# A written-out order of some 5,400 operations is replaced by another, and the last tile leaves in one transfer

## The chip, the core and the metric

One NeuronCore of a Trainium2 chip runs the whole program. It has five engines with a queue of instructions each: TensorE (PE, matrix products), VectorE (DVE), ScalarE (ACT), GpSimd (POOL) and SyncE (SP, which here only issues transfers). The metric is the device time of one execution in microseconds, the median of several runs.

## The reference: banded and pooled attention, then a maxout layer

Attention runs over 8 batches, 8 heads, 576 positions of 64 numbers. The local part lets each position see only its neighbours at a distance under 4. The pooled part averages q, k and v over groups of 4 positions, runs full attention on the 144 averages, and repeats each result 4 times. Their sum, 4608 tokens of 512 numbers, goes through three products, their elementwise maximum, and an output product.

```python
q_d = q.reshape(B, H, Sd, factor, D).mean(axis=3)      # factor 4, Sd 144
out_d = sm_attn(q_d, k_d, v_d)
out_up = np.repeat(out_d, factor, axis=2)
mask = np.abs(pos[:, None] - pos[None, :]) < factor
scores = np.where(mask, scale * np.matmul(q, k.transpose(0, 1, 3, 2)), -1e9)
out_local = np.matmul(softmax(scores), v)
x = (out_up + out_local).transpose(0, 2, 1, 3).reshape(B * S, H * D)
h = np.maximum(np.maximum(x @ w1, x @ w2), x @ w3)     # 512 -> 768
return h @ w_out                                       # 768 -> 512
```

## The kernel before

**The work.** The tokens are cut into nine blocks of 512: the first 512 positions of each of the eight batches (blocks 0 to 7), and block 8, the last 64 positions of all eight. A block's attention is done in two groups of four heads, n = 2j and 2j+1. In blocks 0 and 1 the local attention runs on PE, in windows, with two head pairs a group; from block 2 on DVE, POOL and ACT do it by products, sums over seven offsets and multiplications. Two chains of the first part matter here. In `wide_scores` (L1264) PE opens two score banks with the mask (operations 24 and 25, 44 and 45, 84 and 85), adds the scores (26, 46, 86), DVE takes maxima, ACT exponentials, DVE sums and reciprocals (37 to 39), and one last multiplication in two halves (60 and 61 for the second pair of group 0, 124 and 125 for the first pair of group 1). In `wide_values` (L1308) PE transposes the result (64 to 67 and 69 for that pair, 174 to 179 for the other), a copy brings it to SBUF, and PE multiplies by v (71). `band_load` (L1133) brings the operands of a later group into tiles that are free by then: by the list `HOMES` (L64) both pairs of group 3 use the tile wlo4, so the loads 366 and 367 wait for the last readers of what lay there (the value products 383), the scores 389 read them, and the loads 369 and 370 of the next pair wait for 389 before the scores 390 can start. Pooled attention has its scores 132 to 139 and others, its pd transposes (489 waits for ptail, written by 483) and its products (454).

The maxout layer works with numbers split into a high and a low part; a product is three matmuls of 128x128 by 128x512 (`layer_one`, L1355). `mlp_column` (L1374) makes one of six columns of a block's hidden layer, `mlp_out` (L1400) its four output tiles y of 128 tokens: eighteen matmuls into one PSUM bank, a copy, a transfer to DRAM. Blocks 7 and 8 go through the maxout products together. There are four banks of tag pm, three of pa and one of pq.

**The order.** The kernel first records its operations as numbers, in the order in which the Python code names them, with what each needs (class Recorder); then `emit` (L723) issues them. Which engine does an operation and in what order stands in `TABLE` (L79), a list of words: a number or a range and a letter for the engine (P for PE, D for DVE, A for ACT, G for POOL, S for SP). `340D` is operation 340 on DVE, `24-25P` are 24 and 25 on PE. A word with F asks for so many filler matmuls: `20F` are 20 bf16 matmuls of the mask tile into a free bank, whose result nobody reads (`warm`, L705). `follow` (L617) goes through the list word by word and gives each new tile a place in SBUF or PSUM, the one that came free first by its own reckoning of times (`take`, `opens`, `ready`). So the list sets the order of each of the five queues and, through the places, who waits for whom.

```python
        for o, e in turn:
            if o is None:
                self.free[e], self.last_kind = self.warm(self.free[e]), "B"
                continue
            t = max(self.free[e], self.ready(o, e))
            for tag, infos in self.opens(o).items():
                places = sorted(self.freed[tag])[: len(infos)]
                assert len(places) == len(infos), (o.key, tag)
```

All instructions are issued by one line at the end of `emit`, L769, so the profile tells them apart by tile and shape only; which operation a row belongs to follows from its place in its engine's queue. Fillers show as rows whose only source is prod, 128x448 bf16. A load or store in the profile is a DMA named by its tile (v_1_0 and v_1_2 are loads of v for group 1, k_4_0 of k for group 4, traw_2_0 and rawin_1_1 of a tail and of a piece of w_in).

Of the kernel before, what the change touches and what calls it, by code (L numbers as in the profile page):

```python
# [79 lines left out]
11D 6S 8D 2D 4D 18D 3D 9S 5D 0D 7A 1D 10S 340D 884-885D 13-14S 126S 12S 129S 24-25P 167S 44P 21D 45P 169S 1F 26P 22D 19-20S 62D 42S 27D 46P 63D 28A  # L80
127G 16S 29-30A 17S 128G 34D 31A 47D 132P 43S 130G 32A 54D 33A 133P 197S 131G 48A 55D 134P 49A 168G 248S 50A 35D 135P 56A 140D 136-137P 170G 138-139P
51A 141D 52A 23S 142D 53A 171D 143A 36A 57D 238S 144A 58-59D 145A 60D 240S 61D 146A 6F 64-65P 37D 147A 66P 253S 73D 67P 69P 148A 258S 68A 74D 172G 70A
263S 149D 6F 71P 150D 155A 157D 278S 154D 173D 198G 152A 341S 151A 160P 199G 161P 72A 156D 162P 38D 158-159P 39D 163P 249D 165-166A 40D 200S 164A 41D
4F 75-76P 153D 1F 77P 15D 78P 250D 80P 84P 79A 85-86P 81A 342S 251A 82P 239D 87D 252D 268S 88A 105P 89A 106-107P 94D 241G 90A 346S 91A 83A 192P 95D
108D 242G 92A 115D 109A 203P 93A 288S 205P 116A 254D 193A 211D 194-195A 293D 196A 204P 110A 206P 111A 207-210P 112A 212D 296D 310S 113-114A 117A 213D
118A 214A 255D 315S 119A 259D 120-121A 260D 215A 96A 386S 122-123D 363D 216A 124G 97A 511S 217A 125D 20F 174P 414S 175P 98A 201D 176P 218A 177P 364D
202G 179P 449S 99A 219A 178D 100A 220D 180A 294A 221D 6F 181P 101-102D 451S 226D 228A 103G 225D 223A 227D 222D 104D 231P 297A 232P 229P 224D 295D 230P
# [1679 lines left out]
```

## Time and profile before

| what | us |
| --- | --- |
| median of 3 runs (690.0 to 691.69) | 690.52 |
| the profiled execution, its own time | 690.0 |
| its span in the trace | 688.2 |
| PE busy in the span | 675.5 (98%) |
| DVE busy | 627.1 (91%) |
| ACT busy | 400.9 (58%) |
| POOL busy | 361.9 (53%) |

The span is what the trace shows from the first to the last instruction; 1.8 us of the execution's time lie around it. A busy engine is not a useful one: the fillers count as busy. An engine's idle time matters only where it holds up the engine that the end hangs on.

### The profile page before, as it was taken

Reading aid. Unit: us, or ns where it says so; the run is one execution under the profiler, and the core shown is the slowest. Engines: PE = TensorE matmul, PEld = TensorE weight load, DVE = VectorE, ACT = ScalarE, POOL = GpSimd, SP = SyncE. Lnnn points to the kernel's source line nnn. Section 1 sums busy time; section 2 is a strip of 40 time slices with the busy share of each in tenths; the row PEclk is TensorE's granted clock in tenths of the full one; section 3 lists DMA queues with packets and bytes.
Section 4 is the critical chain, followed back from the end, with each engine's and each line's share of the span. In section 5 each row is a group of like instructions: output and inputs, shape, how many; then the busy total and the mean of one; then the engine's idle time right before and its main releaser. Section 6 shows DMA issues by size and latency. Waiting matters only on the chain.

```text
span 688.2 us, 12559 instructions
## 1 busy us (share of the span) xinstructions
PE 675.5 (98%) x4277; PEld 542.4 (79%) x4277; DVE 627.1 (91%) x855; ACT 400.9 (58%) x1352; POOL 361.9 (53%) x581
## 2 busy tenths in 40 slices
PE   6999999999999999999999999999999999999997
PEld 4678777878787788778877887788878888888885
DVE  7999999999999999999999999999998898999620
ACT  5875565658488547846684767556685654434121
POOL 2213137879599686839684968558356313332000
PEclk9999999999999999999999999999999999999999
DMA  9997455845355555445464635333430010000012
GB/s 307 402 314 234 130 166 183 241 129 191 114 159 170 176 173 165 140 145 171 155 172 133 188 121 158 85 112 108 146 98 19 1 61 1 1 0 1 1 61 61
DMA packets 50178, 92.79 MB, mean 135 GB/s; under 512 B 5540, under 2 KB 19426, under 8 KB 50114
## 3 DMA queue, kind: packets, MB, share of 16 engines
q1 hardware_dynamic: 49978, 91.86, 42.3%
q8 instruction: 33, 0.54, 0.3%
q14 instruction: 31, 0.25, 0.1%
q10 hardware_dynamic: 136, 0.13, 0.1%
HBM read 82.53 MB, written 9.44 MB: 134 GB/s over the span
## 4 chain that ended last, share of the span: by engine, by line
PE 89%; DVE 5%; ACT 2%; DMA 1%; issue 1%; SPq 0%; DVEq 0%
PE pm L769 75%; PE pa L769 13%; PE pq L769 2%; ACT prod L769 1%; DMA wlo<-in_kt_dense_dram 1%; ACT pa L769 1%; DMA whi<-in_qt_dense_dram 1%; DVE wlo_0r L769 1%; DVE t L769 0%; DVE hqk L769 0%; DVE sums L769 0%; DVE hh L769 0%; DVE xlo_0r L769 0%; DVE prod L769 0%; DVE qkT L769 0%
## 5 line engine op out<-in xcount | busy, mean ns | idle before, releaser
L769 PE MATMUL pm<-xlo_0r,whi_0r 128*128 128x512 f32 x540 | 211.8, 394 | 0.3 <-DVE xlo_0r L769 0.3
L769 PE MATMUL pm<-xhi_0r,wlo_0r 128*128 128x512 f32 x540 | 211.5, 392 | 0.0
L769 PE MATMUL pm<-xhi_0r,whi_0r 128*128 128x512 f32 x540 | 211.2, 392 | 0.0
L769 ACT ACTIVATE pv<-v,sums 128x64 f32<-128x64 f32 x532 | 140.2, 414 | 28.0 <-DVE x L769 11.0
L769 POOL TENSOR_TENSOR pv<-v,sums 128x256 f32<-128x256 f32 x245 | 145.5, 700 | 6.3 <-DMA v<-in_v_dram 2.9
L769 PE MATMUL pm<-wo_0r,hh_0r 128*128 128x512 f32 x576 | 137.8, 393 | 0.0
L769 PEld LDWEIGHTS pm<-wo_0r,hh_0r 128*128 128x128 f32 x576 | 106.7, 188 | 22.4 <-issue 0.6
L769 PEld LDWEIGHTS pm<-xlo_0r,whi_0r 128*128 128x128 f32 x540 | 101.3, 188 | 22.8 <-issue 2.0
L769 PEld LDWEIGHTS pm<-xhi_0r,wlo_0r 128*128 128x128 f32 x540 | 101.4, 188 | 21.0 <-issue 0.5
L769 PEld LDWEIGHTS pm<-xhi_0r,whi_0r 128*128 128x128 f32 x540 | 101.4, 188 | 20.9 <-issue 0.6
L769 DVE TENSOR_TENSOR prod<-k,pq 128x1792 f32<-128x1792 f32 x56 | 112.2, 2004 | 0.5
L769 DVE TENSOR_REDUCE sums<-prod 128x28 f32<-128x1792 f32 x56 | 112.0, 2001 | 0.3
L769 DVE TENSOR_REDUCE x<-pv 128x256 f32<-128x1792 f32 x43 | 85.9, 2008 | 1.3 <-POOL pv L769 1.2
L769 ACT COPY y<-pm 128x512 f32<-128x512 f32 (+1 forms) x48 | 27.9, 585 | 50.8 <-PE pm L769 38.5
L769 ACT CAST hh_0r<-pm 128x512 fp32r<-128x512 f32 x47 | 27.8, 591 | 40.3 <-DVE pm L769 40.3
L769 POOL TENSOR_TENSOR x<-whi_0r,wlo_0r 128x512 f32<-128x512 f32 x16 | 22.8, 1437 | 47.4 <-DVE x L769 32.4
L769 POOL TENSOR_TENSOR pv<-pv 128x768 f32<-128x768 f32 (+1 forms) x26 | 40.4, 1552 | 2.2 <-ACT pv L769 1.1
L769 ACT COPY pq<-q 128x256 f32<-128x256 f32 x56 | 22.1, 395 | 25.9 <-DVE prod L769 23.3
L769 DVE TENSOR_TENSOR hh_0r<-pm,hh_0r 128x512 fp32r<-128x512 f32 x47 | 32.0, 681 | 1.6 <-ACT hh_0r L769 1.4
L769 POOL TENSOR_TENSOR hv<-v 128x128 f32<-128x128 f32 (+1 forms) x53 | 26.7, 513 | 12.7 <-DMA v<-in_v_dram 12.5
L769 DVE TENSOR_TENSOR pm<-pm,t 128x512 f32<-128x512 f32 x44 | 30.4, 691 | 2.7 <-PE pm L769 2.4
L769 ACT COPY t<-pm 128x512 f32<-128x512 f32 x42 | 24.9, 592 | 13.6 <-PE pm L769 13.3
(377 smaller groups left out, 1035.1 us busy)
## 6 DMA issues: line engine op xcount, KB each, us to landing
k<-in_k_dram SPq DMA_DIRECT2D x55, 320.0 KB
v<-in_v_dram SPq DMA_DIRECT2D x54, 320.0 KB
out_dram<-y SPq DMA_DIRECT2D x35, 256.0 KB
q<-in_q_dram SPq DMA_DIRECT2D x56, 128.0 KB
hqk<-in_qt_pool_dram SPq DMA_DIRECT2D x24, 256.0 KB
hqk<-in_kt_pool_dram SPq DMA_DIRECT2D x24, 256.0 KB
wo<-in_w_in_dram SPq DMA_DIRECT2D x8, 511.8 KB
hh<-in_w_in_dram SPq DMA_DIRECT2D x6, 511.8 KB
```

Of the source, the lines that this page charges most:

```text
L769: getattr(self.engines[o.eng], method)(*map(real, args), **{k: real(x) for k, x in kw.items()})
```

## The change

Three things change. `TABLE` is another list. In `follow` a filler is issued only if a bank of pm or pa is free at that place of the list. And `mlp_out` no longer cuts the last tile, y_8_3, in two (before: ACT copies the left half and issues its transfer, DVE copies the right half and SP issues its transfer); ACT copies it whole and SP sends it, as all others. Two operations fall away with that, 5390 and 5391.

```diff
@@ -629,7 +612,8 @@
         assert len(asked) == known == len(set(asked)), "the table is of another program"
         for o, e in turn:
             if o is None:
-                self.free[e], self.last_kind = self.warm(self.free[e]), "B"
+                if self.freed["PSUM", "pm"] or self.freed["PSUM", "pa"]:
+                    self.free[e], self.last_kind = self.warm(self.free[e]), "B"
                 continue
             t = max(self.free[e], self.ready(o, e))
             for tag, infos in self.opens(o).items():
@@ -1407,16 +1391,12 @@
             for m, (a, b) in enumerate(ops):
                 pe.matmul(ps, a, b, start=m == 0, stop=m == len(ops) - 1)
             y = new([P, DM], tag="y", bufs=2, name=f"y_{j}_{f}")
-            pieces = 2 if (j, f) == (B, FAC - 1) else 1
-            w = DM // pieces
-            for x in range(0, DM, w):
-                last = x > 0
-                (dve.tensor_copy if last else act.copy)(y[:, x : x + w], ps[:, x : x + w])
-                if j < B:
-                    dst = dram(out, (j * S + f) * DM + x, [[FAC * DM, P], [1, w]])
-                else:
-                    dst = dram(out, (FAC * P + f) * DM + x, [[S * DM, B], [FAC * DM, TAIL], [1, w]])
-                (act if pieces > 1 and not last else sp).dma_start(dst, y[:, x : x + w])
+            act.copy(y, ps)
+            if j < B:
+                dst = dram(out, (j * S + f) * DM, [[FAC * DM, P], [1, DM]])
+            else:
+                dst = dram(out, (FAC * P + f) * DM, [[S * DM, B], [FAC * DM, TAIL], [1, DM]])
+            sp.dma_start(dst, y)
 
```

The two lists begin as follows (the old one with its first nine lines of 193, the new one with its first seven of 176):

```diff
-11D 6S 8D 2D 4D 18D 3D 9S 5D 0D 7A 1D 10S 340D 884-885D 13-14S 126S 12S 129S 24-25P 167S 44P 21D 45P 169S 1F 26P 22D 19-20S 62D 42S 27D 46P 63D 28A
-127G 16S 29-30A 17S 128G 34D 31A 47D 132P 43S 130G 32A 54D 33A 133P 197S 131G 48A 55D 134P 49A 168G 248S 50A 35D 135P 56A 140D 136-137P 170G 138-139P
-51A 141D 52A 23S 142D 53A 171D 143A 36A 57D 238S 144A 58-59D 145A 60D 240S 61D 146A 6F 64-65P 37D 147A 66P 253S 73D 67P 69P 148A 258S 68A 74D 172G 70A
-263S 149D 6F 71P 150D 155A 157D 278S 154D 173D 198G 152A 341S 151A 160P 199G 161P 72A 156D 162P 38D 158-159P 39D 163P 249D 165-166A 40D 200S 164A 41D
-4F 75-76P 153D 1F 77P 15D 78P 250D 80P 84P 79A 85-86P 81A 342S 251A 82P 239D 87D 252D 268S 88A 105P 89A 106-107P 94D 241G 90A 346S 91A 83A 192P 95D
-108D 242G 92A 115D 109A 203P 93A 288S 205P 116A 254D 193A 211D 194-195A 293D 196A 204P 110A 206P 111A 207-210P 112A 212D 296D 310S 113-114A 117A 213D
-118A 214A 255D 315S 119A 259D 120-121A 260D 215A 96A 386S 122-123D 363D 216A 124G 97A 511S 217A 125D 20F 174P 414S 175P 98A 201D 176P 218A 177P 364D
-202G 179P 449S 99A 219A 178D 100A 220D 180A 294A 221D 6F 181P 101-102D 451S 226D 228A 103G 225D 223A 227D 222D 104D 231P 297A 232P 229P 224D 295D 230P
-233P 182A 234P 183-185P 888S 186P 237A 298D 188P 236A 187A 189D 264D 896S 235A 256A 5F 190P 265D 261A 257D 269D 266A 243P 886S 191A 262D 347P 546P
...
+6S 11D 8D 2D 4D 18D 3D 9S 5D 0-1D 10S 340D 884-885D 7A 13-14S 126S 12S 129S 24-25P 167S 44P 21D 45P 169S 22D 1F 26P 19-20S 62D 42S 46P 27D 16S 127G
+63D 17S 128G 28-29A 43S 34D 130G 30A 132P 197S 47D 31A 131G 133P 32A 54D 168G 248S 134P 33A 135P 55D 48A 170G 49A 136P 35D 137P 23S 50A 138P 141D 140D
+56A 36A 139P 52A 51A 53A 85P 84P 86P 171G 142D 37D 57D 38D 58D 39D 59D 61D 60D 94D 15D 172D 143-146A 173D 40-41G 69P 6F 64-65P 70A 147-148A 95A
+149-150D 157D 87D 66-67P 4F 75-76P 1F 77-78P 73-74G 198-199G 68A 100A 6F 71P 152D 155D 151D 154D 156D 153D 72D 99A 96-97A 79A 98A 160P 158-159P
+161-163P 105P 80P 88-89A 165A 164A 92A 90-91A 93A 249D 166D 250D 81D 251A 207P 106-107P 208-210P 192P 213D 101D 108D 115D 109D 116D 253S 254D 102-103D
+82P 83D 194A 193A 195-196A 112A 118A 117A 119-120A 114A 110-111A 121A 113A 204P 203P 205-206P 258S 259D 211-212D 104G 414S 415D 252D 122D 416D 123D
+260D 124D 268S 200S 240S 238S 125D 214-219A 269A 255D 220D 293D 221D 20F 174P 183-185P 179P 175-177P 186P 180A 178A 222A 294A 256A 187A 261A 225D 296G
...
```

They end as follows; 5299 to 5307 are the last nine matmuls of the tile y_7_3, 5308 and 5309 its copy and transfer, 5374 to 5387 belong to y_8_3:

```diff
-5354-5367P 5370-5371P 5368A 5372-5373P 5369S 5374-5387P 5390D 5388-5389A 5391S
...
+5343-5345P 5372P 5355-5358P 5346-5347P 5348A 5349S 5359P 5373P 5360-5361P 5374P 5362P 5375P 5363-5367P 5368A 5369S 5376-5380P 5297-5298P 5381-5387P
+5388A 5389S 5299-5307P 5308A 5309S
```

PE's list has the same 2843 operations in both, and 49 fillers; 312 operations change the engine (94 go from POOL to ACT, 81 from ACT to POOL, 48 from DVE to POOL, 44 from ACT to DVE, 30 from POOL to DVE, 15 from DVE to ACT).

## Rows read from the trace of the kernel before

**Rows 1.** Busy time by stretch: bounds, length, busy us of each engine, clock, DMA share, GB/s

```profile
11.00:40.00 29.00, 27.96 (x437) 18.49 (x438) 26.76 (x71) 25.46 (x112) 7.66 (x13) 1.00 1.03 388
40.00:72.00 32.00, 30.25 (x511) 24.19 (x510) 30.60 (x59) 18.07 (x31) 7.61 (x9) 1.00 0.77 255
72.00:116.00 44.00, 43.65 (x400) 33.72 (x399) 43.11 (x71) 27.59 (x78) 15.87 (x22) 1.00 0.48 144
116.00:683.00 567.00, 566.98 (x2840) 461.80 (x2839) 519.31 (x635) 325.05 (x1112) 327.87 (x529) 1.00 0.37 113
```

**Rows 2.** Timeline of PE around 11 us: start us, us, engine, line, operation, out<-in, count

```profile
10.91 2.20 PE L769 MATMUL pm<-prod 128*128 128x448 bf16 x6
```

**Rows 3.** Timeline of PE, 25 to 33 us

```profile
25.13 3.96 PE L769 MATMUL pm<-prod 128*128 128x448 bf16 x20
29.46 0.96 PE L769 MATMUL pm<-ident,prod 128*128 128x128 f32 x5 [0.38 <-POOL prod L769]
```

**Rows 4.** Waits of PE over the whole span: us in total, times, longest

```profile
PE pa L769 <- DMA wlo<-in_kt_dense_dram: 1.5, 1, 1.5
PE pm L769 <- ACT pa L769: 0.6, 1, 0.6
PE pm L769 <- POOL prod L769: 0.4, 1, 0.4
PE pm L769 <- DVE xlo_0r L769: 0.3, 1, 0.3
PE pa L769 <- ACT dtail L769: 0.3, 1, 0.3
```

**Rows 5.** Timeline of DVE, 12 to 14 us

```profile
13.15 0.89 DVE L769 TENSOR_TENSOR prod<-prod,zb 128x256 f32<-128x256 f32 x2
```

**Rows 6.** Timeline of PE, 58 to 72 us

```profile
58.18 0.21 PE L769 MATMUL pq<-prod,wlo 32*64 32x18 f32 x2
...
63.56 0.89 PE L769 MATMUL pa<-wlo 64*26 64x32 f32 x80
...
64.72 0.40 PE L769 MATMUL pm<-xhi_0r,wlo_0r 128*128 128x512 f32 x1
...
68.59 0.39 PE L769 MATMUL pm<-xhi_0r,whi_0r 128*128 128x512 f32 x1
70.44 0.86 PE L769 MATMUL pa<-wlo 64*26 64x32 f32 x80 [1.46 <-DMA wlo<-in_kt_dense_dram]
```

**Rows 7.** The chain of waits, 55 to 72 us: start us, us, what

```profile
64.93 5.38 DMA wlo<-in_kt_dense_dram
```

**Rows 8.** Timeline of PE around 108 us

```profile
108.39 0.30 PE L769 MATMUL pa<-ident,pd 128*128 128x128 f32 x1 [0.29 <-ACT dtail L769]
```

**Rows 9.** Groups by line and form: busy us, mean ns, idle time before

```profile
L769 DVE TENSOR_REDUCE x<-pv 128x256 f32<-128x1792 f32 x43 | 85.9, 2008 | 1.3 <-POOL pv L769 1.2
...
L769 POOL TENSOR_TENSOR pv<-pv 128x768 f32<-128x768 f32 x13 | 24.0, 1850 | 1.2 <-ACT pv L769 1.1
...
L769 POOL TENSOR_TENSOR pv<-pv 128x512 f32<-128x512 f32 x13 | 16.3, 1254 | 1.0
```

**Rows 10.** Timeline of DVE, 678 to 689 us

```profile
683.53 0.42 DVE L769 COPY y<-pm 128x256 f32<-128x256 f32 x1 [24.25 <-PE pm L769]
```

**Rows 11.** DMA share, 684 to 688 us, 40 slices of 0.1 us, digits in tenths

```profile
DMA  0000000000004444445555455546510000000000
```

**Rows 12.** Timeline of ACT, 667 to 689 us

```profile
667.20 0.59 ACT L769 COPY y<-pm 128x512 f32<-128x512 f32 x1 [1.79 <-PE pm L769]
...
679.44 0.59 ACT L769 COPY y<-pm 128x512 f32<-128x512 f32 x1 [3.49 <-PE pm L769]
683.99 0.37 ACT L769 COPY y<-pm 128x256 f32<-128x256 f32 x1 [3.96 <-DVE y L769]
```

**Rows 13.** DMA share, 680 to 684 us, as before

```profile
DMA  0000000000001846292503822245553564321000
```

**Rows 14.** DMA share, 667 to 671 us, as before

```profile
DMA  0000000000000000399989940000000000000000
```

More of the change, by code (lines that the diff above doesn't have):

```diff
@@ new lines @@
+1489A 1260A 1235P 955-956P 959A 1236-1244P 1232D 989D 1205A 1044G 999G 1001P 1274-1275P 1289-1292P 1003-1005A 1002A 1093A 1483D 1206D 1245D 1246A
+1096A 1247D 1091A 1051P 1054D 1053D 1052D 1095A 1090A 1276P 1261-1268P 1302P 1293P 1269-1270P 1277-1278P 1271P 1279-1281P 1272P 1490-1491D 1273D
+1282-1285P 1286D 1092G 1102G 1055A 1497A 1056-1060A 1294-1295P 1303-1304P 1296-1300P 1305-1311P 1287A 1104A 1301A 1330-1331P 1315-1318P 1332P
+1061-1062D 1064A 1063A 1496S 1498D 1066D 1068D 1067D 1333P 1072P 1070-1071P 1334P 1633G 1103G 1615-1616G 1100G 1607G 1634G 1608G 1097G 1094G 1598S
@@ new lines @@
+1398-1400P 1375P 1357-1366P 1075P 1453-1454P 1514A 1329D 1515D 1455D 1516D 1603A 1078A 1077A 1456A 1401P 1367P 1376P 1368D 1517G 1564G 1377-1378P
+1411P 1120P 1379P 1412-1415P 1124A 1121A 1380P 1416-1417P 1381P 1610S 2076S 1122A 1369A 1457D 1604D 1370D 1605D 1382P 1465-1466P 1383P 1418P
+1384-1385P 1419P 1431P 1386-1388P 1552S 1557A 1123A 2058S 1609S 1617S 1611A 1554A 1389A 1567A 1467-1468P 1469D 1470A 1559A 1568A 2043G 1555G 1612D
+1458P 1402P 1432-1436P 1403P 1472-1474P 1459-1461P 1475P 1462D 1471D 1476D 1437P 1420P 1404-1408P 1421P 1563G 1553G 1560G 1566G 2059G 1558G 1556G
@@ new lines @@
+1637G 1565G 1561D 1569G 1571G 1618S 1390S 2050S 871S 1422-1425P 1582S 1572S 1409A 1463A 1477A 1478D 2188S 2046S 1410S 1464D 1613D 1426-1428P 1619A
+1429A 1438P 1711-1712P 1714P 1713P 1715-1716P 1720P 1717P 1583G 1721P 1737P 1439-1445P 1722P 1446-1448P 1738P 1524P 1585A 1587A 1575A 1589A 1576A
+1449A 1620D 1526-1527D 1525D 1621D 1574G 2077G 1590G 1578-1579G 2078G 2060G 1573G 1584G 2044G 1580G 1625D 2051G 1626D 1739-1748P 1726-1728P 1732P
+1718P 1752P 1719P 1753P 1733-1734P 1723-1725P 1577A 1588A 1581D 1586A 2052G 1627G 1528-1533A 1628A 1729-1731P 1754P 1735A 1591D 1450S 2037S 2039A
@@ new lines @@
+1693G 1696G 1708G 2214G 2224G 1710G 2191S 2648S 2184S 2632S 2142S 2183S 2649G 1699G 1656D 2057D 2064-2065D 2069D 1875P 1868-1869P 1876-1877P
+1889-1891P 2185A 1859D 2070D 1870P 2082P 1892P 1878-1884P 1893-1897P 1885P 1871P 2226G 2633G 2227G 2634G 2199S 2152S 2079S 2071G 2080-2081G 1886P
+1901-1904P 1898-1899P 2186-2187D 2196S 2192S 2086A 1872D 1887A 2072A 2193A 2085A 2073D 2194D 2640S 1873A 2074D 1874D 1900D 1916-1918P 1905-1911P
+2087-2089P 1919-1920P 1912P 1921-1924P 2084A 2201A 1913D 1925P 1929P 1926-1927P 2115D 2195D 2075G 2197G 2149A 1928A 1930-1933P 1942P 1957P 2117D
@@ new lines @@
+3461G 3462A 3825A 3319A 3316-3318P 3321A 3293A 3294D 3826-3827D 3477G 3475G 3197-3198P 3481P 3492P 3189P 3320A 3476A 3471A 3464A 3482P 3190P 3496P
+3199-3201P 3497P 3202-3208P 3408P 3483P 3176S 3832S 3953S 3831S 3156S 3480G 3472G 3463G 3473-3474G 3479G 3410A 3409A 3833A 3415D 3413D 3467A 3469G
+3414D 3416-3418A 3209-3214P 3912S 3922S 3961S 3954S 3992S 3851G 3215A 3419-3420A 3412A 3487-3489P 3493-3495P 3499-3501P 3505A 3411A 3834-3835D
+3191-3193P 3955A 3421A 3498P 3507-3508P 3194P 3195A 3509-3510P 3502P 3511-3513P 3503P 3522-3523P 3514-3515P 3524P 3516P 3525-3526P 3504P 3517P
```

330 lines of the change are left out of this document (147 added, 183 removed).

## Prediction, made before the changed kernel was run

> **What bounds the kernel now.** I first read the busy time of each engine in six stretches, four of which matter [rows 1]. From 116 to 683 us TensorE (PE) is busy 566.98 of 567.00 us: whatever the other engines do there is covered, and the end moves only by what PE does in the first 116 us, by a new PE wait later, and by what follows its last matmul. From 11 to 116 us the same column leaves 1.0, 1.8 and 0.4 us idle. Busy is not useful, though: of the 29 us from 11 to 40, PE spends some 10 on matmuls that fill waits (the table's F words, rows with prod as the only source): six in 2.20 us at 10.91 and twenty in 3.96 us at 25.13 are the two ends of it [rows 2, 3]. So what can be won is the waits, and fills only where the list has fewer of them.
>
> The second view is who made PE wait [rows 4]: 1.5 us for a load into wlo, 0.6 us for a softmax, 0.4 us for POOL's product, 0.3 us each for the operand xlo and for a softmax tail. Beside these 3.1 us the view has only the waits for the first loads, before 11 us.
>
> **The change, part by part.** I read both tables as five queues, one per engine, and added the durations of the trace along them. PE's list holds the same 2843 operations and 49 fills, so PE's work is the same; some 310 operations go to another engine.
>
> *0 to 11 us.* PE's first fourteen operations, SP's first eighteen and DVE's first twenty-two stand as they did: 0.
>
> *11 to 40 us.* (a) Operation 60, half of a softmax's last multiplication, now stands on DVE behind 37, 38, 39 and 61 (1.41 us together) and no longer behind 171 (0.41 us, to POOL). It ended within the pair of 13.15 to 14.04 us [rows 5]; it ends 1.0 us later, and the transposes 64 to 67 of PE with it. In their place PE is given 85, 84 and 86, the three score operations of the next head pair, which stood after both groups of this pair's transposes and need nothing new: the time is used, not lost. (b) The next gate is operation 124, then 125: the product before the second group of transposes, for which PE waits at 29.46 us [rows 3]. Up to 125 DVE is given 16 operations of 6.25 us (score maxima, pd, pt, xb copies from ACT) and loses 11 of 5.99 us (to POOL, or to later places): 0.26 us more. Product 124 itself goes from POOL to DVE, where the pair of [rows 5] took 0.89 us together. PE has 20 fills ahead of it in both lists, so it stands there again, 0.2 us later. (c) One fill of the 49 falls out: at the second 1F all four pm and all three pa banks are held in list order, and the new condition skips it; 0.19 us, but PE then waits for 124 anyhow: 0. (d) SP's loads change places from the nineteenth on, while the DMA engines are full, 1.03 of their time [rows 1]; what is brought forward (traw_2_0, rawin_1_1) pushes v_1_0 and v_1_2 back by two loads, and their reader on DVE has itself gone back 34 places: 0. Sum +0.2 us; at best the waits of 0.6 and 0.4 us and the xlo wait beside them go (-1.3), at worst the 1.0 us of (a) comes back whole (+1.2).
>
> *40 to 72 us.* The wait for wlo is a chain of its own: the value products 383 end at 58.39 us and free the tile, two loads follow, and PE's scores 389 start at 63.56; they free the tile again, the second pair of loads ends in one that goes out at 64.93 and takes 5.38 us, and scores 390 start at 70.44 [rows 6, 7]. What PE has in hand meanwhile counts. Before: 21 matmuls and two 0.14 us bank openings, then 19 matmuls. After: 19, then 22, and the openings stand elsewhere. From start to start these take 0.228 us (17 from 64.72 to 68.59) [rows 6]. So the cover is 9.4 us before (40 matmuls and the openings) and 9.3 after (41). The first chain lasts 5.1 us, up to 389, if it only just came in time, as I take it. It is then no longer covered (4.3 us of matmuls: a new wait of 0.8), and the second wait shrinks from 1.46 to about 0.9: +0.2 us. Bounds: the first loads land early, within the cover that is left, and the second wait goes too (-1.6); or the k_4_0 load that now stands ahead of the second pair in SP's list takes its bandwidth (+1.0).
>
> *72 to 116 us.* The transposes 489 wait 0.29 us at 108.39 us [rows 8]. Before them stand 4.3 us more of PE work in the new list, and 1.1 us less of DVE work up to their last reader 483: the wait goes. The matmul before could have been followed 0.45 us earlier; with 0.15 us of the same kind at the products 454: -0.6 us. Bounds 0 and -0.9.
>
> *116 to 683 us.* Twelve sums over seven offsets go from DVE's one reduction, 2.01 us, to POOL's three additions, of which the first two take 1.85 + 1.25 us, all three some 4; 94 and 81 multiplications trade between POOL and ACT [rows 9]. DVE is freed of some 24 us of 519 and POOL gets 48 more on 328 of 567 [rows 1]: neither is near the end. PE reads what these sums make 8 us later at the least, most of it 40 us. 0; at worst one such wait for a late sum each in two blocks, +1.5.
>
> *The end.* Now PE ends with the tile y_8_3, and that leaves in two halves: DVE's copy starts at 683.53 us, ACT's follows (it reads the same bank), and the two transfers' last packets start at 686.9 to 687.0 us [rows 10, 11]. After, the list ends otherwise: y_8_3 is done nine matmuls, 2.05 us, before the last one, and those nine finish y_7_3, whose copy by ACT and transfer by SP stand last. Both go in one piece. Their prices are there: y_8_2, of y_8_3's form, is copied in 0.59 us by 680.03 and has its last packets at 683.6 to 683.7, 3.65 us later; y_7_3 itself is copied by 667.79 and has its last at 669.3 to 669.4, 1.55 us later [rows 12 to 14]. So y_8_3 ends at 683.53 - 2.05 + 0.59 + 3.65 = 685.7, and y_7_3, were it alone, at 683.53 + 0.59 + 1.55 = 685.7 too. They meet: y_8's rows keep the DMA engines less than half busy as a mean, y_7's 0.9 of them for 0.8 us [rows 13, 14], which I read as eight of sixteen against all. What y_7_3 has for those eight stands behind y_8_3 and adds up to 0.8 us; I take 0.7: 686.4 instead of 687.0, -0.6 us. Bounds -1.3 (they pass without touching) and +0.1 (the meeting costs twice that). One piece as such is no gain: the halves needed 3.0 us from the start of the second copy, 683.99 [rows 12], the whole 3.65 from the end of its one. [...]
>
> **Sum** against the profiled execution's own 690.0 us (688.2 of span and 1.8 around it): +0.2 + 0.2 - 0.6 + 0 - 0.6 = -0.8, 689.2. The median of the runs, 690.52, lies 0.5 above that execution, so I put the measured time at 689.7 us.
>
> **Rivals.** *The clock comes late (slower).* Fills at 10.91 us take 0.37 us each and those at 25.13 us 0.20 [rows 2, 3]: the first run at half speed, the 1.2 GHz level, though the column prints 1.00 there. PE was busy without a break ahead of that rise. In the new list it has 85, 84 and 86 there, then stands still for over a microsecond until operation 61 is done, and the fills come only behind 69. If it is still at the low level then, the 16 fills between 69 and 71 cost 0.17 us more each, 2.7 us, and pass it on through the copies of 71's banks to DVE and so to 124: 689.7 + 2.7 = 692.4. It decides if the fills behind 69 take 0.37 us. For it: that idle time. Against it: 84 to 86 are work too. The Trainium skill, TensorE: Matmul & The Clock Gate, Part 1, says that the slow clock is the resting state and that sustained activity lifts it; the trace agrees. Chance 0.13.
>
> *The load chain and the softmax waits go (faster).* If the wlo loads land early the 1.6 us go instead of +0.2, and with the 1.3 us of the stretch before instead of +0.2: 689.7 - 3.3 = 686.4. For it: the same pair one block earlier found an emptier queue, and DMA share falls to 0.77 in that stretch [rows 1]. Against it: the cover in matmuls is the same. Chance 0.25.
>
> *A new wait inside the covered stretch (slower).* Long accumulations now interleave over all four pm banks: operation 812 opens an output tile some 19 us of PE work early, and near the end 5310 opens y_8_0 only some 0.3 us after DVE's 5229 frees its bank, by the same sums. At a place like that one operation in the way, of 0.59 us as ACT's copies [rows 12], holds PE by 0.3 us or more; I count seven with less than 0.3 us to spare in the new list, one in the old: with 0.35 us at each, 689.7 + 2.5 = 692.2. It decides if the whole operation is in the way at each. Against it: the list has that room, and DVE is free 48 us of 567. Chance 0.1.
>
> **How the numbers follow.** The forecast, no change that can be told, has 0.52; its own range is the sum of the bounds taken as independent, 687.2 to 691.9. A measurement of this kernel tells about 0.3% (2.1 us) from no change: 688.4 to 692.6. The forecast gives 0.09 to faster and 0.02 to slower; the second rival's 0.25 goes to faster; the first and the third, at the edge of that band, give 0.11 of their 0.23 to slower and the rest to the same. That makes 0.34, 0.53 and 0.13. The range reaches from the second rival to the first: 686.3 to 692.5.
>
> **What would show it.** Right: PE's idle time before 390's scores split into two waits near 63 and 70 us; no wait at the pd transposes near 108; PE unbroken from 116 us; the last packets 2.9 us behind the last matmul. Wrong: fills of 0.37 us behind 14 us; a PE wait after 116 us; both wlo waits gone; last packets later than 3.3 us behind the last matmul.

## The result and the profile after: 1.2% slower, where no change was forecast

The changed kernel took 699.1 us as a median of 4 runs (696.01 to 699.88); the kernel before, beside it, 690.26 (689.3 to 691.69). The ratio is 1.0118 [1.0083, 1.0153]. The forecast was 689.7 us, the range 686.3 to 692.5: the measured time lies outside of it, on the slow side. The profiled execution shown here took 699.88 us with a span of 698.1, against 690.0 and 688.2 before.

The busy time of each engine by stretch, for the changed kernel; the columns are those of [rows 1]:

```profile
11.00:40.00 29.00, 26.82 (x353) 18.02 (x353) 26.04 (x74) 22.33 (x101) 8.97 (x13) 0.94 0.72 256
40.00:72.00 32.00, 31.15 (x590) 24.61 (x588) 28.91 (x55) 16.16 (x29) 6.90 (x7) 1.00 0.86 290
72.00:116.00 44.00, 41.06 (x361) 31.58 (x362) 40.56 (x70) 23.19 (x68) 21.15 (x26) 1.00 0.55 179
116.00:692.50 576.50, 573.28 (x2876) 460.61 (x2875) 512.37 (x646) 334.20 (x1148) 377.93 (x558) 1.00 0.36 112
```

PE (second number) is idle 2.2 us from 11 to 40 (1.0 before), 0.9 from 40 to 72 (1.8 before), 2.9 from 72 to 116 (0.4 before) and 3.2 behind 116 us (0.02 before). The clock of the first row is 0.94, not 1.00. Who made PE wait, from the view of waits (us in total, times, longest):

```profile
PE pm L753 <- DVE t L753: 3.3, 2, 2.6
PE pm L753 <- DMA prod<-in_band_dram: 3.1, 1, 3.1
PE pm L753 <- ACT pa L753: 1.9, 1, 1.9
PE pm L753 <- issue: 1.4, 1, 1.4
...
PE pm L753 <- DVE hh_0r L753: 1.2, 1, 1.2
PE pa L753 <- DVE qkT L753: 0.5, 1, 0.5
```

Against [rows 4]: the load into wlo (1.5) and the wait of 489 are gone. The second line is the first load, before 11 us, which the old kernel has too. The softmax's (third line) has grown from 0.6 to 1.9, and five new ones of half a microsecond or more have come: two on DVE's t, one on its hh_0r, one put down to its qkT, and one for nothing that is seen.

**At 14 us.** PE's timeline, then those of DVE and POOL, of the changed kernel:

```profile
11.25 0.79 PE L753 MATMUL pm<-pv 64*58 64x64 f32 x36
13.93 0.30 PE L753 MATMUL pm<-ident,prod 128*128 128x128 f32 x1 [1.89 <-ACT pa L753]
14.07 1.78 PE L753 MATMUL pm<-prod 128*128 128x448 bf16 x6
15.64 1.06 PE L753 MATMUL pm<-ident,prod 128*128 128x128 f32 x4
16.50 1.70 PE L753 MATMUL pm<-prod 128*128 128x448 bf16 x4
```
```profile
12.83 1.97 DVE L753 TENSOR_TENSOR prod<-prod,zb 128x384 f32<-128x384 f32 x2
```
```profile
12.80 1.71 POOL L753 TENSOR_TENSOR prod<-prod,zb 128x256 f32<-128x256 f32 x2 [1.13 <-DVE zb L753]
```

The transposition 69 starts 1.89 us after the score operations are through. The view names ACT, but what 69 reads is the half that operation 61 writes, the first of DVE's pair at 12.83 us. That pair took 0.89 us in the old kernel [rows 5], where POOL ran nothing from 12.43 to 14.82 us (its next operation there is the first line below); here POOL does 40 and 41 in the same two microseconds, and the pair takes 1.97, of which 61 alone 1.00 instead of 0.55. The sixth experiment (e6, below) has the new order at this place, but 40 and 41 on DVE behind the pair; there POOL is idle beside it, and the pair takes 0.89 again (second line).

```profile
14.82 0.46 POOL L769 TENSOR_TENSOR th<-traw 128x128 f32<-128x128 f32 x1 [2.39 <-DMA traw<-in_qkt_tail_dram]
```
```profile
13.57 0.89 DVE L753 TENSOR_TENSOR prod<-prod,zb 128x384 f32<-128x384 f32 x2
```

Behind the standstill the clock falls (stretch by stretch, clock in the third column from the end):

```profile
14.00:16.00 2.00, 2.00 (x9) 1.19 (x10) 2.00 (x5) 1.14 (x6) 1.92 (x4) 0.69 1.04 412
16.00:18.00 2.00, 2.00 (x9) 1.13 (x8) 1.93 (x7) 1.26 (x6) 1.44 (x4) 0.50 1.00 400
18.00:20.00 2.00, 2.00 (x19) 1.25 (x19) 0.59 (x5) 1.77 (x10) 0.00 (x0) 0.96 0.98 324
```

From 14.7 us PE runs 3.4 us at 0.50, the lower level, and the four fills at 16.50 take 0.37 us each to the next start.

**From 62 to 96 us**, PE's timeline:

```profile
64.12 1.14 PE L753 MATMUL pa<-wlo 64*26 64x32 f32 x80 [0.50 <-DVE qkT L753]
...
70.42 0.87 PE L753 MATMUL pa<-wlo 64*26 64x32 f32 x80
...
72.40 0.50 PE L753 MATMUL pm<-xhi_0r,whi_0r 128*128 128x512 f32 x1 [0.68 <-DVE t L753]
...
79.93 2.06 PE L753 MATMUL pa<-y,whi 32*64 32x26 f32 x128
81.82 0.63 PE L753 MATMUL pa<-prod,whi 32*64 32x26 f32 x32
82.38 0.73 PE L753 MATMUL pm<-xhi_0r,wlo_0r 128*128 128x512 f32 x2
84.50 0.39 PE L753 MATMUL pm<-xlo_0r,whi_0r 128*128 128x512 f32 x1 [1.39 <-issue]
...
94.98 0.50 PE L753 MATMUL pm<-wo_0r,hh_0r 128*128 128x512 f32 x1 [1.16 <-DVE hh_0r L753]
```

At 64.12 the scores 389 wait, as forecast (put down to DVE's qkT here; 0.6 us and put down to the load into wlo in e5, a second run of the same kernel). At 70.42 the scores 390 no longer wait at all, where about 0.9 us was forecast. Not forecast: 669 at 72.40 and 812 at 94.98 open a PSUM bank that DVE has yet to give back, and at 84.50 operation 700 stands 1.4 us with nothing to wait for that the profile shows ("issue"), two matmuls behind a burst of 160 small ones (410 and 411). What DVE does ahead of 812's bank:

```profile
90.26 2.01 DVE L753 TENSOR_TENSOR prod<-k,pq 128x1792 f32<-128x1792 f32 x1
92.31 2.02 DVE L753 TENSOR_REDUCE sums<-prod 128x28 f32<-128x1792 f32 x1
94.24 0.68 DVE L753 TENSOR_TENSOR hh_0r<-pm,hh_0r 128x512 fp32r<-128x512 f32 x1
```

The last of these is 709, the reader of the bank; the list puts 890 and 891 before it, 4 us of work.

**At 400 us**, DVE, POOL and PE:

```profile
396.55 4.02 DVE L753 TENSOR_TENSOR sums<-sums,mask 128x48 f32<-128x48 f32 x1
400.49 0.15 DVE L753 TENSOR_SCALAR rd<-pa 128x5 f32<-128x5 f32 x1
400.56 0.67 DVE L753 TENSOR_TENSOR t<-pm,t 128x512 f32<-128x512 f32 x1
```
```profile
396.26 0.75 POOL L753 TENSOR_TENSOR kd<-hqk 128x256 f32<-128x256 f32 x1
...
399.77 0.73 POOL L753 TENSOR_TENSOR vd<-hv 128x256 f32<-128x256 f32 x1
```
```profile
401.29 0.50 PE L753 MATMUL pm<-xhi_0r,whi_0r 128*128 128x512 f32 x1 [2.61 <-DVE t L753]
```

An operation on 48 columns (3395) is on record with 4.02 us while POOL runs seven operations without a break, and DVE's next reader of a PSUM bank, 3080 at 400.56, comes too late for PE. It is a single event: of nine other traces with this stretch of the list, the same operation took 0.20 us in eight and 0.74 in one.

**The end**, ACT's last copy and the DMA share from 694 to 698 us, 40 slices of 0.1 us:

```profile
693.96 0.58 ACT L753 COPY y<-pm 128x512 f32<-128x512 f32 x1 [1.45 <-PE pm L753]
```
```profile
DMA  7382421822346478999895464532000000000000
```

The last packets start at 696.7 us, 2.8 to 2.9 behind the last matmul's end at 693.88, as forecast. The trace ends 4.23 us behind that end; before it was 4.77 (683.44 to 688.21). The last matmuls after, then before:

```profile
691.68 2.20 PE L753 MATMUL pm<-wo_0r,hh_0r 128*128 128x512 f32 x9
```
```profile
679.65 3.79 PE L769 MATMUL pm<-wo_0r,whi_0r 128*128 128x512 f32 x16
```

**Where the time went.** PE is on the path nearly everywhere, so I took, from one PE operation's start to the next one's, what went beyond the time that the same operation took in the old trace (0.229 us at most for a 128x512 matmul, 0.19 for a fill) and added it up by stretch. A wait counts where the operation before it starts, in the time of its own trace: 669's, at 71.2 us in after and 71.3 in e5, stands in the row 40 to 72. Column e5 is the changed kernel run once more, unaltered; the other columns are experiments of the next section.

| us of PE beyond the work | before | after | e5 | e9 | e10 | e11 | e13 | e15 | e3 | e12 |
| --- | --- | --- | --- | --- | --- | --- | --- | --- | --- | --- |
| 0 to 11 | 1.9 | 1.8 | 1.9 | 2.5 | 2.0 | 1.6 | 2.3 | 3.4 | 1.9 | 1.5 |
| 11 to 40 | 2.5 | 3.9 | 3.9 | 2.5 | 5.0 | 3.2 | 2.9 | 1.9 | 2.5 | 2.7 |
| 40 to 72 | 3.2 | 3.1 | 3.3 | 3.7 | 5.1 | 3.6 | 3.6 | 3.1 | 3.2 | 2.1 |
| 72 to 100 | 1.0 | 4.0 | 4.6 | 4.9 | 3.3 | 5.9 | 3.1 | 4.6 | 1.1 | 2.3 |
| 100 to 116 | 1.1 | 0.4 | 0.3 | 0.6 | 0.4 | 0.4 | 0.5 | 0.3 | 1.1 | 0.8 |
| behind 116 | 6.9 | 14.2 | 11.8 | 11.0 | 10.9 | 11.0 | 11.9 | 9.6 | 10.8 | 6.9 |
| sum | 16.6 | 27.4 | 25.8 | 25.3 | 26.8 | 25.7 | 24.3 | 22.9 | 20.5 | 16.4 |

The sums close: after, 27.4 - 16.6 and -0.5 at the end make 10.3, where the two profiled executions differ by 9.9; for e5 9.2 - 0.6 = 8.6 against 8.4. The event at 400 us makes 3.1 us of after's last row (3.65 us from 380 to 410 us, against 0.55 in e5).

### The profile page after: what moved, and what is told of

Same layout as the page of the kernel before. It is cut to its first block, busy times and chain, and to the rows that moved or that the text cites. A ratio compares the mean times of both kernels' runs of the same rounds, so it can differ in the third digit from the quotient of the medians.

```text
span 698.1 us, 12535 instructions
## 1 busy us (share of the span) xinstructions
PE 680.2 (97%) x4276; PEld 539.8 (77%) x4276; DVE 615.1 (88%) x865; ACT 401.2 (57%) x1363; POOL 418.1 (60%) x612
## 5 line engine op out<-in xcount | busy, mean ns | idle before, releaser
L753 PE MATMUL pm<-xhi_0r,whi_0r 128*128 128x512 f32 x540 | 204.3, 397 | 3.5 <-DVE t L753 3.3
L753 PE MATMUL pm<-xhi_0r,wlo_0r 128*128 128x512 f32 x540 | 205.8, 394 | 0.0
L753 PE MATMUL pm<-xlo_0r,whi_0r 128*128 128x512 f32 x540 | 202.0, 395 | 1.4 <-issue 1.4
L753 ACT ACTIVATE pv<-v,sums 128x64 f32<-128x64 f32 x576 | 154.7, 415 | 14.2 <-DVE x L753 5.6
L753 POOL TENSOR_TENSOR pv<-v,sums 128x256 f32<-128x256 f32 x234 | 149.1, 708 | 15.1 <-DMA v<-in_v_dram 10.7
L753 PE MATMUL pm<-wo_0r,hh_0r 128*128 128x512 f32 x576 | 152.2, 398 | 1.2 <-DVE hh_0r L753 1.2
L753 POOL TENSOR_TENSOR pv<-pv 128x768 f32<-128x768 f32 (+1 forms) x48 | 74.4, 1549 | 10.7 <-ACT pv L753 8.5
L753 DVE TENSOR_REDUCE x<-pv 128x256 f32<-128x1792 f32 x32 | 64.1, 2009 | 3.7 <-PE pa L753 2.1
L753 ACT COPY y<-pm 128x512 f32<-128x512 f32 x49 | 28.6, 589 | 50.7 <-PE pm L753 43.7
L753 DVE TENSOR_TENSOR t<-pm,t 128x512 f32<-128x512 f32 x43 | 29.1, 678 | 4.2 <-PE pm L753 4.0
```

The lines of the kernel that those rows point to most:

```text
L753: getattr(self.engines[o.eng], method)(*map(real, args), **{k: real(x) for k, x in kw.items()})
```

## The experiments

Times are medians; ratios are to the kernel before, run on the same chip. The edits are in words of the lists.

**One piece on the old list (e1).** Only `mlp_out` and the last words change.

```diff
-5354-5367P 5370-5371P 5368A 5372-5373P 5369S 5374-5387P 5390D 5388-5389A 5391S
+5354-5367P 5370-5371P 5368A 5372-5373P 5369S 5374-5387P 5388A 5389S
```


> The old list with only the new end of mlp_out: y_8_3 copied whole by ACT and sent by SP in one transfer; y_8_3 is still the last tile. By the term of the prediction one piece is no gain: last packets at 683.53 + 0.59 + 3.65 = 687.8 instead of 687.0, so +0.8 us (691.0). [...] That the end explains the loss of the new kernel would need +9.

Measured: 690.87 against 689.9, 1.0014 [1.0004, 1.0023]. The whole tile costs 0.97 us more than the two halves; its last packets start 3.6 us behind the end of its copy. So the gain at the end is the list's, which finishes another tile last.

**The changed kernel again, and 3080 ahead of 3395 (e5, e4).**

```diff
-3083-3092P 3054D 3395D 3304D 3080D 3305D
+3083-3092P 3054D 3080D 3395D 3304-3305D
```


> The changed kernel once more, for what varies from run to run. If the 4.02 us of DVE's 3395 and the 2.6 us that PE waits behind it belong to the list, they are there again; if they were a meeting of that one run (in the third and fourth experiment 3395 took 0.20 us), they are gone, and the time is still 696 to 700. PE's waits at 11 to 14, 71, 83 and 94 us (2.1, 1.0, 1.6 and 1.3 us) should be there in any case; a stretch of 3.4 us with the clock at 0.50 behind the first of them is there in some runs.

> The new list with one operation moved two places: DVE's 3080, the last reader of the bank that PE waits for at 398.7 us, goes ahead of 3395, the product of 4.02 us that stood in its way. If PE waits because 3080 is queued behind 3395, the wait of 2.61 us goes and the time is 699.1 - 2.6 = 696.5, while 3395 still takes about 4 us. If the bank comes free late for another reason, the wait stays and the time is 699.1.

Measured: e5, with no edit, 699.16, 1.0139 [1.0115, 1.0163]; e4 699.6, 1.0133 [1.0112, 1.0154]. In both traces 3395 took 0.20 us and 380 to 410 us lost 0.5 us, not 3.7. The order at that place is not what the median pays for; e4 says nothing more.

**Splices (e2, e3, e11).** e2 goes by the new list for PE's first 122 us and by the old one from there; e3 by the old for 255 us; e11 by the old for 41 us. The seam of e3, against the old list:

```diff
-2092A 2202D 2146G 1946-1947P 2147G 2148A 1948-1950P 2149G 1951P 2153A 1952-1953P 2154G 1957P 2093D 2162S 1958P 2155G 2156A 1959P 2628S 1954D
+2092A 2202D 2146G 1946-1947P 2147G 2148A 1948-1950P 2149G 1951P 2153A 1952-1953P 1957P 2117D 2116D 2157G 2159G 2156G 2158A 2118-2119A 1958-1962P 2093D
...
```


> The new list up to PE's operation 862 (about 122 us), then what is left in the order and on the engines of the old one; one piece at the end. Theory A (the loss is made of separate PE waits, each where the new list puts it): the first 122 us of the new trace hold 3.8 us of excess over the old one, with 0.7 for the end: 690.3 + 4.5 = 694.8. Theory B (a late start upsets the order of all that follows, so that the later waits come from the first stretch): all of it, 699. Theory C (the loss is in the later stretches alone): 691.

> The old list up to PE's operation 1953 (about 255 us), then the new one to the end, with y_7_3 as its last tile. Theory A: 6.7 us of excess after 255 us less 0.5 at the end: 696.5, with the wait of 2.6 us for the bank of ph_4_4_1 near 398 us in it. Theory B: about 690, since it starts as the old one does. Theory C: 699.

> The old list up to PE's operation 190 (about 41 us, all the fillers), the new one from there. The wait of 2.1 us that the new list puts before 69 and the fall of the clock to 0.50 behind it can't be there: 11 to 40 us then hold 2.5 us of excess over the plain sum of PE's work as in the old kernel, not 3.9, so 697.7; and PE's waits from 63 to 95 us stay, if they are the new list's own. If these come from the late start, they go too: 693 or less.

Measured: e2 701.63, 1.0172 [1.0155, 1.0189]. Its seam made a loss of its own (11.0 us from 116 to 380, before 4.5), so as a price of the front it is worthless; its front showed the same waits as after, this time without a fall of the clock. e3: 695.18, 1.0077 [1.0054, 1.0099]: with the front as before, the rest of the new list still costs 5.3 us in the median. Its four executions are two of 693.9 us, at a mean clock of 0.998, and two of 696.5 and 696.8, at 0.996; the trace is one of the first, and has 3.9 us more than before behind 116. e11: 700.83, 1.0153 [1.0127, 1.0178]: 69 no longer waits, but PE stands 1.6 us ahead of 64 in its place, at 13.7 us, since the old list's six fills ran at the full clock there and were over sooner; 64 starts at 13.66 us, before at 13.67. The clock stays up behind it and falls at 85.6 us instead, and the median is no better than e5's.

**Order and engines apart (e6, e7).** e6 has the new order with every operation on its old engine, e7 the old order with the new engines. One line of each:

```diff
-56A 36A 139P 52A 51A 53A 85P 84P 86P 171G 142D 37D 57D 38D 58D 39D 59D 61D 60D 94D 15D 172D 143-146A 173D 40-41G 69P 6F 64-65P 70A 147-148A 95A
+56A 36A 139P 52A 51A 53A 85P 84P 86P 171D 142D 37D 57D 38D 58D 39D 59D 61D 60D 94D 15D 172G 143-146A 173D 40-41D 69P 6F 64-65P 70A 147-148A 95D
...
-51A 141D 52A 23S 142D 53A 171D 143A 36A 57D 238S 144A 58-59D 145A 60D 240S 61D 146A 6F 64-65P 37D 147A 66P 253S 73D 67P 69P 148A 258S 68A 74D 172G 70A
+51A 141D 52A 23S 142D 53A 171G 143A 36A 57D 238S 144A 58-59D 145A 60D 240S 61D 146A 6F 64-65P 37D 147A 66P 253S 73G 67P 69P 148A 258S 68A 74G 172D 70A
```


> The order of the new list, with every operation on the engine that the old list gives it. Theory E (the 312 operations that change the engine are the loss, above all the 56 us of work that POOL gets): back to 691 or less. Theory O (the order is the loss: what stands in front of what in the queues of PE and DVE): no better than the new kernel, 697 to 703, with PE's waits of the first 100 us still there.

> The order of the old list, with every operation on the engine that the new list gives it; one piece at the end. Theory E: as the new kernel, 697 or more. Theory O: near the old list with one piece, 691 to 693.

Measured: e6 768.62, 1.1139 [1.1121, 1.1156]; e7 722.79, 1.0488 [1.046, 1.0515]. Each half alone is far worse than both together. Order and engines were chosen for each other, and these runs do not price either.

**The stop at 84 us (e8, e10).** e8 puts seven matmuls between 409 and the burst 410 and 411; e10 puts the burst five matmuls earlier.

```diff
-689P 698P 690-691P 407A 410P 409A 411P
+689P 698P 690-691P 407A 692P 699-701P 693P 702-703P 410P 409A 411P
...
-696-697P 689P 698P 690-691P 407A 410P 409A 411P
+696P 407A 410P 409A 411P 697P 689P 698P 690-691P
```


> The new list with seven matmuls of the first layer (692, 693 and 699 to 703) moved ahead of 410 and 411, the 160 small matmuls that PE runs through in 2.4 us just before it stops for 1.4 to 1.9 us without a semaphore to wait for. In the trace the stop ends when a packet of instructions has landed. If PE stops because the instructions behind the burst are fetched too late, 1.6 us more work between request and need takes most of the stop away, 1.4 us and, where the clock fell behind it, up to 3: 697.5. If the stop is a wait for data that the trace doesn't name, it stays: 699.1.

> The new list with the 160 small matmuls 410 and 411 five matmuls earlier (ahead of 697, 689, 698, 690, 691). The eighth experiment moved them seven later, and the stop behind them stayed, 1.6 us. If the stop is at a fixed number of PE's instructions (an instruction packet that is asked for when the one before it is begun, and the burst runs through that one too fast), five matmuls now lie between the burst and the stop, 1.1 us more: it shrinks from 1.4 to 1.9 us to 0.3 to 0.8, and the time to 698. If it follows the burst, it stays 1.4 us or more right behind 411.

Measured: e8 699.65, 1.0138 [1.0123, 1.0154]. The stop stays, 1.6 us beyond the work, and now stands inside 411, ahead of the last five small matmuls of the burst:

```profile
85.43 0.30 PE L753 MATMUL pa<-prod,whi 32*64 32x18 f32 x5 [1.33 <-issue]
```

Counted from the start of the trace, that is ahead of the same matmul as in after: the 1239th, whichever operation it belongs to. So it is in all eight traces that have the stop (after, e2, e4, e5, e8, e9, e11, e15). e10 698.54, 1.0105 [1.008, 1.0131]: the stop is gone; the 1239th matmul stands eighth behind the burst there, where it is third in after. So the stop hangs on how far behind the burst that place in PE's stream of instructions lies, not on an operand. The time hardly moved; in the traced execution 389 waited 2.4 us and the clock fell twice, at 13.4 and 68.0 us.

**The banks back (e9).**

```diff
-324D 682P 516S 888S 369-370S 521S 655P 647-649P 656-661P 650P 624P 625D 651-652P 653D
+682P 516S 888S 369-370S 521S 655P 647-649P 656-661P 650P 624P 651-652P 653D 324D 625D
...
-890D 708A 452G 530G 450G 519A 520G 927G 763A 426-429A 667A 891D 709D
+708A 709D 890D 452G 530G 450G 519A 520G 927G 763A 426-429A 667A 891D
```


> The new list with four operations moved: DVE's 709, the last reader of the bank that PE waits for at 94 us, goes ahead of the 4.06 us of 890 and 891 (and ACT's 708 before it), and 653, the last reader of the bank of 669, ahead of 324 and 625. If PE waits there because DVE's queue holds the banks' readers back, PE's waits before 669 (1.0 to 1.3 us) and 812 (1.3 to 1.7 us) go in the trace: 699.1 - 2.5 = 696.6. If these banks come free late by other causes, both waits stay.

Measured: 698.45, 1.0126 [1.0095, 1.0156]. Its waits:

```profile
PE pa L753 <- DMA wlo<-in_kt_dense_dram: 1.9, 1, 1.9
PE pm L753 <- issue: 1.6, 1, 1.6
PE pm L753 <- ACT pa L753: 1.5, 1, 1.5
```

Both DVE lines are gone: giving the bank's reader its old place removes the waits of 669 and 812, which shows their cause. (389 waited longer than in e5 here, which alone gives DVE time; but of e11 and e13 below, where it waited 1.1 us in both, e11 has the waits of 669 and 812, 1.2 and 1.3 us by the table's measure, and e13, with these moves, has neither.) The time did not follow: the loads for 389 became the wait (1.9), and the clock fell at 85.0 us, during the stop.

**All of the front's moves undone at once (e13)**: e11, e9 and e10 together, the edits as above.

> Old list to 41 us, then the new one with the moves of the ninth and the tenth experiment together: the wait at 11 us, the two waits for banks at 71 and 94 us and the stop behind the burst are all taken away at once. If these four and the falls of the clock behind them are most of the loss, the excess of 72 to 100 us falls from 4.0 to 6.1 us to 1.5, and the time from 700.8 to 694 to 695; what is left above the old list is the wait at 63 us (1 to 2) and the small ones behind 116 us (4.3 us of excess more than the old list there, less 0.5 at the end). If what is taken away comes back elsewhere, it stays at 698 or more.

Measured: 697.0, 1.0111 [1.009, 1.0131]; the clock did not fall in it. 72 to 100 us lost 3.1 us where 1.5 was expected: other waits came in place of those removed.

```profile
PE pm L753 <- DVE hh_0r L753: 1.0, 1, 1.0
PE pa L753 <- DMA wlo<-in_kt_dense_dram: 0.9, 1, 0.9
PE pa L753 <- DMA whi<-in_qt_dense_dram: 0.7, 1, 0.7
```

The first is the next bank of the same kind (723's); behind 116 us all stayed as it was.

**The transpositions together (e15).** The new list breaks transpositions into smaller groups: behind 116 us PE goes from one to another matmul 86 times, 40 before. e15 draws 41 tiles' transpositions together, in the manner of its first places:

```diff
-951P 1226-1227P 1248-1249P 1228P 1202P 1250-1254P 1229-1230P 1487S 1233P 952P
+1226-1227P 1248-1249P 1228P 1202P 1250-1254P 1229-1230P 1487S 1233P 951-952P
...
-1382P 1465-1466P 1383P
+1382-1383P
...
```


> The new list with the transposes of 41 tiles put together again, each group at the place of its last one: 61 changes from a transpose to another matmul instead of 100 (the old list has 50). Behind 116 us the new list is 4.9 us slower than the old in pieces under 0.5 us. The first matmul behind a transpose starts its successor 0.314 us later instead of 0.227. If each change costs these 0.087 us, 39 fewer give 3.4 us back behind 116 us (695.7). If the transpose itself is shorter by as much where it stands alone (0.028 us to the next start instead of 0.110), a change costs 0.02 us, and 0.8 us come back (698.3). If nothing comes back, the pieces are something else.

Measured: 695.45, 1.0083 [1.0066, 1.01], 3.7 us less than e5 in the median, 2.9 between the two traced executions. Between the first and the last of the places edited, the same work took 412.6 us. In e5 it took 414.7, but 413.9 in e4, e8, e9, e10 and e11, which have the unedited list there. So the edit is worth 1.3 us; the other 0.8 are gaps between plain matmuls that e5 has and those five traces don't (over 0.25 us: nine in e5, three in each of the five and in e15). The changes themselves are little. A matmul behind a transposition hands on after 0.315 us, not 0.227, but a transposition ahead of a matmul after 0.028, not 0.109: a change costs some 0.01 us. What else closed up I did not find out. That the median came out near the 695.7 of the first theory is luck.

**Moves from the reading, on the old list (e12, e14).** e12 brings six matmuls ahead of 390 and one ahead of 489, and ends on the tile y_7_3; e14 also puts six matmuls ahead of 403 and takes six of 20 fills out.

```diff
-338A 390P 512A 664P 391D 460D 887S 339G 665P 536S 669-672P 395D 895S 673P 978G 674P
+338A 664-665P 669-672P 390P 512A 391D 460D 887S 339G 536S 395D 895S 673P 978G 674P
...
-806P 906D 1027S 489P 918G 487-488P 490-491P 494A 1013G 492P 807P 493A
+806P 906D 1027S 807P 489P 918G 487-488P 490-491P 494A 1013G 492P 493A
...
-5287P 5290-5291P 5269S 5292-5303P 5288A 5304-5306P 5289S 5307P 5310-5311P 5308A 5312-5313P 5309S 5314-5327P
+5287P 5269S 5288A 5289S 5310-5327P
...
-5374-5387P 5390D 5388-5389A 5391S
+5374-5387P 5388A 5389S 5290-5307P 5308A 5309S
```

What e14 adds to it:

```diff
-97A 511S 217A 125D 20F 174P 414S 175P
+97A 511S 217A 125D 14F 174P 414S 175P
...
-687P 903S 688P 402D 403-404P 689P 666D 405-406P 408P 690P
+687P 903S 688P 402D 689P 695-699P 403-404P 666D 405-406P 408P 690P
```


> The old list with three things moved by what the traces showed: six matmuls (664, 665, 669 to 672) ahead of the scores 390, whose load comes late (wait of 1.5 us); 807 ahead of the transposes 489 (0.3 us); and y_7_3, copied and sent in one piece over all sixteen DMA engines, behind y_8_3 as the last tile, so that the transfers of 3.65 us that use half of the engines are hidden. If each wait is only what PE has no work for: -1.4, -0.2 and at the end 685.7 instead of 687.0, -1.3: 687.2, below both kernels. If the load of 390 comes later by as much as PE does, or the end hangs on something else, it is 690.

> The kernel of the twelfth experiment (688.9) with two more moves: six matmuls (689, 695 to 699) ahead of the transposes 403, for which its PE stood 1.3 us, and six of the twenty fillers ahead of 174 left out, so that the 160 small matmuls behind 403 keep their place in PE's count of instructions. If the wait at 403 is only missing work: 688.9 - 1.3 = 687.6. If 403 comes later by as much, 688.9. If PE's count matters and is upset, a stop of 1 us or more behind the burst: 690; and a clock at 0.50 behind 29 us, where the fillers are gone, would add 1.5.

Measured: e12 688.93 (688.38 to 690.26), 0.9978 [0.9967, 0.9989]; e14 688.82, 0.9982 [0.9973, 0.9991]. Both beat both kernels, by 1.2 and 1.3 us against the kernel before beside them. Of the two waits that e12 takes away, 390's came back at another place:

```profile
PE pa L770 <- DVE prod L770: 1.2, 1, 1.2
...
PE pa L770 <- issue: 0.2, 1, 0.2
```

The 1.5 us ahead of 390 are gone, and 403 stands 1.2 us at 76.2 us instead; ahead of 489 hardly anything is left, and 100 to 116 us lose 0.3 us less. The gain is the end's: the trace ends 3.66 us behind the last matmul (686.94 behind 683.28), before 4.77. Here y_8_3 is done eighteen matmuls before the last one, and its transfer is no longer in the way of y_7_3's. In e14 403's wait is gone and two others came, 1.1 us more ahead of 174 and 1.1 at 82.5 us: nothing was gained over e12.

## Why the prediction was wrong, step by step

The sum forecast -0.8 us; the two traced executions of the changed kernel took 8.4 (e5) and 9.9 us (after) more than the one before.

*11 to 40 us: the step that failed is (a), "the time is used, not lost"; +0.2 was put, +1.4 came.* Operation 60 did end about when forecast, at 14.80 us. But 85, 84 and 86 are through at 12.04 us, and the transposition 69, which waits for 61, then stood 1.89 us. I had priced 60 and 61 from a row beside which POOL stood idle; with 40 and 41 at work there they take 1.97 us, not 0.89, and e6 shows that it is POOL's work that does it. Of the 1.89 us, some 0.45 are that: 61 goes first and took 1.00 instead of 0.55. The Trainium skill, SBUF — State Buffer, section "Who interferes with whom", says that a DVE instruction with two inputs in SBUF contends with a GpSimd instruction that reads SBUF; this pair agrees with it, 1.97 us against 0.89. Moving work to POOL thus had a price on DVE that I did not count. The standstill by itself is not the 1.4 us, though, since PE in the old list filled the same time with matmuls that nobody reads. From 0 to 40 us the old kernel loses 4.4 us by the table's measure. e2, e8 and e9, with the new front, stand 1.5 to 1.9 us ahead of 69, keep the clock up behind it and lose 4.5, 4.5 and 5.1; after, e4, e5, e10 and e15, where the clock falls, lose 5.7, 6.0, 5.7, 7.1 and 5.2. So most of the loss comes with the clock, which the first rival had and the sum had not. Here is e8 at 69: the same standstill, then six fills of 0.19 us to the next start.

```profile
14.24 0.30 PE L753 MATMUL pm<-ident,prod 128*128 128x128 f32 x1 [1.87 <-ACT pa L753]
14.38 1.30 PE L753 MATMUL pm<-prod 128*128 128x448 bf16 x6
```

*40 to 72 us: the size came out, -0.1 (after) and +0.1 (e5) where +0.2 was forecast, but by luck.* The two waits that were forecast, 0.8 us at 389 and 0.9 at 390, came as one, 0.7 at 389, so that the loads cost 0.9 to 1.0 us less than before. In their place PE waited 1.0 (after) and 1.3 us (e5) at 669 for a bank that no term of the sum had. Nor was 389's wait fixed: by the measure of the table it was 0.6 (e2) to 2.4 us (e10).

*72 to 116 us: the term -0.6 failed; it came out at +2.3 (after) and +2.9 (e5).* The wait of 489 went, and 100 to 116 us gained the 0.7. But I followed 489's operands only, and not who gives PE its banks back: 812 waited 1.3 (after) and 1.7 us (e5) beyond its work for DVE, as 669 did in the stretch before, and e9 shows that moving DVE's order there takes exactly these away. The other piece, 1.5 (after) and 1.8 us (e5), is the stop behind the burst. No view of waits gives a releaser for it. But the kernel's own reckoning of times has a term of this kind that I did not look at: its class Fetch lets PE past every 256th instruction only when a set time has gone by since the place 256 before it.

*116 to 683 us: the term 0 failed; +4.9 in e5.* The engines' sums (DVE and POOL far from full) were right, and say nothing on single releases. Three late banks at 627 to 637 us make 1.5 us with the gaps behind them, 1.3 go in e15, 0.8 are gaps that e4, e8, e9, e10 and e11 don't have, and the rest, 1.3 us, is in small pieces that I could not assign. In the profiled execution 3.1 us more came by the single event at 400 us.

*The end: right.* -0.6 forecast, -0.5 measured; the price of one piece 0.97 by e1, where 0.8 was expected.

*The rivals.* The first, the clock, came as described, fills of 0.37 us behind a standstill, but not in every run, and at 68 or 85 us too. It is a part of the spread from 696 to 702 us in the changed lists (e9: 696.44 us at a mean clock of 0.998, 702.29 at 0.990), but not all of it (e11: 702.83 at 0.997). The third, late banks, was the right mechanism, naming 812 too; I put it behind 116 us, and its price of 2.5 us was too small (669, 812 and those at 627 to 637 us came to 3.8 us in after, 4.4 in e5). The two were taken as alternatives, with 0.13 and 0.1, and both happened; but their prices together, 5.2 us, make only 694.9. The stop and the small pieces behind 116 us had no rival. Of the second only part came: the waits for the loads shrank by 1 us, and the softmax wait was replaced by a longer one.

*What stays open*: what the stop at 84 us is, some 1.3 us behind 116, and why the clock falls behind one standstill and not behind another.

## What to carry to other kernels

With five in-order queues a list move is not priced by the operands of what it moves: for every PSUM bank that PE opens, look up the engine that reads it last and what now stands ahead of that reader. Where PE is the bound, taking a wait away mostly uncovers the next one (e9, e12, e13, e14); the saving that stayed whole in these runs was the one at the end itself, as with the last tile. An operation moved to POOL must be priced at what DVE runs beside it. And a term that comes out right in size is not yet a term that is understood: from 40 to 72 us one wait took another's place.

## What the runs showed of the hardware that I had not expected

- PE can stand 1.3 to 1.7 us with no semaphore to wait for. It was ahead of the 1239th matmul of the trace in eight traces, behind or inside a burst of 160 small matmuls, and gone with the burst five matmuls earlier. In the trace's DMA records a transfer in 16 KB packets on the queue q8, of kind instruction, ends at 83.20 us (after) and 84.21 (e4), and PE goes on 1.3 and 1.4 us later; over the eight traces it is 1.25 to 1.47 us, and the next such transfer starts 1.05 to 1.15 us behind that. (So the stop does not end when a packet lands, as e8's expectation read it.) In e10 the 1239th matmul comes 1.6 us behind the end of such a transfer without having to stop. The old trace has such transfers too (its last ends at 83.51), without a stop. The page of after lists 33 of them, one for 259 of PE's 8,552 matmuls and weight loads (`q8 instruction: 33, 0.54, 0.3%`). I read it as the supply of instructions; that is argued, not shown. The Trainium skill, Runtime: NRT & Kernel Launch, section "Instruction fetch mechanics", says that instructions are fetched in 16 KiB blocks and that crossing a block's boundary is mostly hidden; if the reading holds, it was not hidden here.
- One DVE operation of 0.20 us was on record with 4.02 us while POOL ran seven operations on end, in one of ten traces of that stretch; it ended within 0.1 us of POOL's last one. The pair at 12.83 us waited for one POOL operation at a time; this one would have waited through seven. That POOL is the cause here is argued from this one trace.
- With standstills of PE of 1.3 to 2.2 us the granted clock fell to 0.50 for 3.4 us (after at 14.7 us, e8 at 86.8, e9 at 85.0), or 6.8 us (e10 at 13.4), but not always: e2 has the standstill ahead of 69 and no fall, and e5 fell behind that one alone and not behind its stop of 1.6 us. e8 kept its clock through 1.87 us at 14 us and 1.93 at 64, and lost it behind 1.33 us at 85.
